# Row-tile sessions: two steps' scores joined round pieces of a plain down projection and round the first two up products of a row block

## The chip, the core and the metric

The kernel runs on one core of a Trainium2 chip. The metric is the device time of one execution in microseconds (us). The kernel before takes 957.05 us, the median of three runs (956.88 to 957.99). All matrices are f32; on the chip an f32 matmul shows as two records.

## The reference, cut to what matters

Routed attention over 4 batches, 8 heads, 768 positions and head size 64, and then a feed-forward block on its output seen as 3072 rows by 512 columns:

```python
q_assign = np.argmax(np.einsum('bhsd,hcd->bhsc', q_n, c_n), axis=-1)   # 16 clusters; q_n, c_n normalised
k_assign = np.argmax(np.einsum('bhsd,hcd->bhsc', k_n, c_n), axis=-1)
mask = q_assign[:, :, :, None] == k_assign[:, :, None, :]
scores = np.where(mask, scale * np.matmul(q, k.transpose(0, 1, 3, 2)), -1000000000.0)
attn = softmax(scores)                     # exp, then division by the sum of the row
x = np.matmul(attn, v)                     # (B,H,S,D), turned into (3072, 512)
h = x @ w_in                               # 512 by 2048
out = (h - np.tanh(h)) @ w_out             # 2048 by 512
```

## The kernel before, in words

**Steps.** The attention is cut into 96 steps, numbered by `at`. A step is a pair of heads `n` (16 pairs, 4 to a batch), a half of the query columns (384) and a third `s` of the key rows (two key tiles of 128). For a step, `begin` (L492) multiplies keys by queries into two `sc` tiles (L499), and ScalarE takes the exponential in place (L521, written back into `sc`). `select` (L524) multiplies each `sc` tile by the cluster mask on VectorE and writes the weights `e` (L531, two instructions to a tile). GpSimd adds the weights up for the softmax's sum (L543, L547). `value` (L549) multiplies values by weights into `av` (L556). After the third step of a half, `take` copies `av` out on ScalarE (L581), and `total` or `total_both` brings the sum onto all partitions with a matmul into `den`. Later `scale` (L692) or `divide` (L707, L710) multiplies the attention's output `xT` by the reciprocal.

**Pieces.** The feed-forward work of an earlier batch is cut into pieces which a planner lays between the steps. Each has a cost, and a step takes pieces off the front of the list `fill` into `now` while the cost spent keeps pace with the steps. Batch 0 is done in two halves by `plain_items`. Its second half (in steps 24 to 47) has up products and then twelve `project` pieces (L746): four quarters `i` of the 2048 rows of `w_out` for each of three row tiles `sub`. Here a piece is written (sub, i). Batches 1 and 2 (steps 48 to 71 and 72 to 95) are done by `strassen_items`: a seven-product scheme with 8 row blocks `i` of 7 up products `k_` (L933, 56 pieces), and then 21 `down_product` pieces (L1038). An up product is written (i, k_). Batch 3 follows behind the last step.

**Shape of the array.** With f32 and two 64-wide halves, most matmuls split the output's 128 columns of the array in two (written 128*64 in the profile: here "column shape"). The scores have only 64 rows to sum over and split the array's rows (64*128: "row shape").

**Sessions.** From step 49 on, at odd steps at which the piece at the head of `now` is a down product, the flag `joint` (L1261) is set. Then `begin` of the next step, `select` of the next step, that down product with its rows split (`rows_=True`: two partial outputs `parts`, one for each 64 rows, added on VectorE at L1044 or L1053) and `begin` of the step after it stand one behind the other. This document calls such a stretch of row-shaped matmuls a session. At all other steps `begin(following)` stands alone, ahead of `value(at)` and the pieces.

**Order.** The kernel writes the order of every engine's work by hand: an instruction's place in its engine's queue is its place in the code. What a step has to do beside its pieces stands in the list `todo`. It holds the `select` of the next step, the transpose `pq` of the cluster codes by TensorE with the copy `qc` (`publish`, L432, L434), the routing of a later pair on VectorE (`similar`, `turn_back`, `route`: L376, L386 to L414), `scale`, and sums of weight quarters (`made`, L831) for the seven-product scheme. The function `between`, called inside each piece, emits a share of it. Where `now` is empty it is emitted at once. `right_factors` (L899) makes the differences `diff` of `xT` at the start of a batch's pieces.

**Buffers.** PSUM has two `sc` tiles of two banks each, one bank for `av` (pool `ps_a`), and three banks in pool `ps_f` for everything else: up products, down products, `den`, `pq`, `sim` and the accumulator of a plain projection, which keeps its bank for four pieces. There are two `e` tiles (`ep`), so that `select` of a step waits for `value` two steps earlier. `row` tiles (the codes spread over the partitions, L454) number three, and weight blocks (`stream`, L853) three. `fetch_factors` asks for a block two blocks ahead, at product (i, 2).

```python
joint = at > 4 * HALF and at % 2 == 1 and at + 2 < len(steps) and now and now[0][1] == 2
...
elif following and at >= NS - 1 and following not in begun:
    begin(following)
```

Of the kernel before, what the change touches and what calls it, by code (L numbers as in the profile page):

```python
# [30 lines left out]
F32 = mybir.dt.float32  # L31
# [4 lines left out]
ALU = mybir.AluOpType  # L36
# [3 lines left out]
P = 128  # L40
# [18 lines left out]
def kernel(  # L59
# [10 lines left out]
    nc = tc.nc  # L70
# [108 lines left out]
    def fast():  # L179
# [539 lines left out]
        def plain_items(half: int):  # L719
            gs, acc = {}, {}  # L720
            sequence = [i * FQ + o for i in ORDER for o in range(FQ)]

            def up(f: int, between):
                i, o = f // FQ, f % FQ
                if f < CF // 2:
                    gs[f] = gp.tile([P, 2, TB], F32, name="g")
                h = ps_f.tile([P, TB], F32, name="h", tag="f")
                for c in range(CD):
                    for r in halves:
                        nc.tensor.matmul(  # L730
                            h[r], lhsT=w_in[i][:, c, o * P : (o + 1) * P][:, r], rhs=xT[c][:, half],
                            start=(c == 0), stop=(c == CD - 1),
                        )
                th = thp.tile([P, TB], F32, name="th")
                nc.scalar.activation(out=th, in_=h, func=ACT.Tanh)
                between()
                nc.vector.tensor_tensor(
                    out=gs[f % HF][:, f // HF], in0=h, in1=th, op=ALU.subtract
                )

            def project(sub: int, i: int, between):
                if i == 0:
                    acc[sub] = ps_f.tile([P, DM], F32, name="o", tag="f")
                for f in sequence[i * FQ : (i + 1) * FQ]:
                    for r in halves:
                        nc.tensor.matmul(  # L746
                            acc[sub][r], lhsT=gs[f % HF][:, f // HF, sub * P : (sub + 1) * P][:, r],
                            rhs=w_out[f // FQ][:, f % FQ],
                            start=(f == sequence[0]), stop=(f == sequence[-1]),
                        )  # L750
                between()
                if i == NQ4 - 1:
                    osb = restp.tile([P, DM], F32, name="osb", tag="rest")
                    nc.scalar.mul(out=osb, in_=acc.pop(sub), mul=float(words))
                    nc.gpsimd.dma_start(out_r[0, half * HCH + sub], osb)

# [9 lines left out]
            return ups + [  # L766
                (3.4 if half == 0 else 3.0, 1, lambda between, s=s, i=i: project(s, i, between)) for s, i in order
            ]


# [130 lines left out]
        def up_items(b: int, base: int, quarter, shrink, done):  # L901
# [2 lines left out]
            held = {}  # L904
            width = TB if b else TB // 2

            def up_product(i: int, k_: int, between):
                which = PRODUCTS[k_]
                x = [columns(b, c) for c in range(CD)]
                d = diffs[b] if which in (4, 5, 6) else None  # L910
# [13 lines left out]
                        held[i] = t[:, 0, 0:width], t[:, 1].rearrange("p (a n) -> p a n", a=2)  # L924
                s, u = held[i]

                def add(out, x, y):
                    nc.vector.tensor_tensor(out=out, in0=x, in1=y, op=ALU.add)  # L928

                ps = ps_f.tile([P, TB], F32, name="pu", tag="f")[:, 0:width]  # L930
                for c in range(CH):
                    for r in halves:
                        nc.tensor.matmul(  # L933
                            ps[r], lhsT=streams[base + i][:, c, k_, r], rhs=right[c],
                            start=(c == 0), stop=(c == CH - 1),
                        )
                if which == 1:
                    nc.scalar.copy(out=s, in_=ps)
                elif which == 2:
                    add(quarter(i, 0, 0), ps, s)  # L940
                    if i == HF - 1:
                        shrink(i, 0, slice(0, 1))
                elif which == 6:
                    fetch_factors(base + i + 2)
                    add(u[:, 0], ps, s)
                elif which == 7:
                    add(u[:, 1], ps, u[:, 0])
                elif which == 4:
                    add(quarter(i, 1, 0), ps, u[:, 1])
                elif which == 5:  # L950
                    add(u[:, 0], ps, u[:, 0])
                    add(quarter(i, 1, 1), ps, u[:, 1])
                    shrink(i, 1, slice(0, 2))
                else:
                    add(quarter(i, 0, 1), ps, u[:, 0])

                    shrink(i, 0, slice(1 if i == HF - 1 else 0, 2))
# [4 lines left out]


            return [
                (1.3 * width / TB, 1, lambda between, i=i, k_=k_: up_product(i, k_, between))
                for i in range(HF) for k_ in range(len(PRODUCTS))
            ]

# [23 lines left out]
        def strassen_items(b: int):  # L992
# [21 lines left out]
            def down_product(k_: int, j: int, between, rows_=False):  # L1014
# [64 lines left out]


            return up_items(b, base, lambda i, f, t: G[:, i, f, t], shrink, done) + [
                (3.4, 2, lambda between, rows_=False, k_=k_, j=j: down_product(k_, j, between, rows_))
                for k_ in range(len(PRODUCTS)) for j in range(HCH)
            ]

# [152 lines left out]
        for at, (n, half, s) in enumerate(steps):  # L1238
# [19 lines left out]

            joint = at > 4 * HALF and at % 2 == 1 and at + 2 < len(steps) and now and now[0][1] == 2  # L1261
            values_first = 1 in stages and not summed(n, half)
            if values_first:
                value(n, half, s)
# [367 lines left out]
```

## Time and profile before

| | |
|---|---|
| median of three runs | 957.05 us |
| the profiled execution's own time | 955.51 us |
| its span (first to last instruction) | 953.65 us, so 1.86 us lie around it |
| granted TensorE clock | 1.00 |
| busy time of PE (TensorE) / DVE (VectorE) | 939.2 / 580.3 us |
| busy time of ACT (ScalarE) / POOL (GpSimd) | 293.5 / 510.5 us |
| score matmuls L499 | 768 records, 149.3 us |
| plain projection L746 | 384 records, 86.1 us |
| up products L933 | 1792 records, 280.1 us |
| down products L1038 | 2016 records, 223.7 us (191.4 and 32.3) |
| PE, longest waits by releaser | 1.6 us on L531, 1.3 on L231, 1.2 on L581 in all |

PE is the matmul part of TensorE, PEld its weight loads. A timeline line has the start and the time taken in us, engine, source line, operation, output and inputs, shapes, the number of instructions merged (x), and in brackets the idle time ahead of it with what ended it.

### The profile page before, as it was taken

How to read it: one execution, taken by the hardware profiler on the slowest of the kernel's cores; microseconds unless marked ns; L12 is line 12 of the kernel's file. 1: busy time of each engine (PE TensorE's matmuls, PEld its weight loads, DVE VectorE, ACT ScalarE, POOL GpSimd, SP SyncE). 2: the span in 40 equal slices, each digit the busy share in tenths (PEclk: the TensorE clock that was granted, in tenths of full speed). 3: DMA queues.
4: the chain of work that ended last, by engine and by line, in shares of the span. 5: the costliest groups of instructions: out<-in, count | busy, mean ns of one | idle time of the engine just before them, and what ended most of it. 6: DMA issues, size and time to landing. Idle time of an engine off the chain costs nothing.

```text
span 953.6 us, 16953 instructions
## 1 busy us (share of the span) xinstructions
PE 939.2 (98%) x6584; PEld 469.0 (49%) x6584; DVE 580.3 (61%) x1111; ACT 293.5 (31%) x453; POOL 510.5 (54%) x364
## 2 busy tenths in 40 slices
PE   8999999999999999999999999999999999999997
PEld 5434443355653334444465665444456665445664
DVE  6647686976776678566845567766656338443011
ACT  5586564223332332323322112333331220222000
POOL 1026353456775465777785453867797343657500
PEclk9999999999999999999999999999999999999999
DMA  7767465892736645474565645557334223323331
GB/s 193 205 182 154 118 172 128 249 278 86 196 116 160 158 136 132 151 180 132 170 170 182 153 152 187 126 184 170 114 128 147 98 84 100 116 78 132 107 106 37
DMA packets 166764, 139.85 MB, mean 147 GB/s; under 512 B 116580, under 2 KB 145044, under 8 KB 163988
## 3 DMA queue, kind: packets, MB, share of 16 engines
q1 hardware_dynamic: 160292, 117.15, 44.7%
q0 software_dynamic: 6240, 21.50, 6.9%
q8 instruction: 54, 0.88, 0.4%
q14 instruction: 34, 0.28, 0.1%
q10 hardware_dynamic: 144, 0.03, 0.0%
HBM read 117.48 MB, written 21.17 MB: 145 GB/s over the span
## 4 chain that ended last, share of the span: by engine, by line
PE 89%; DVE 3%; DMA 2%; ACT 1%; issue 1%; SPq 0%; DVEq 0%; ACTq 0%
PE pu L933 26%; PE pd L1038 22%; PE sc L499 13%; PE av L556 13%; PE o L746 6%; PE h L730 4%; PE sim L376 1%; PE den L617 1%; DVE e L531 1%; DMA stream<-up_factors 1%; PE den L571 1%; DVE diff L899 1%; PE den L590 1%; DVE den L707 1%; DMA row<-q_codes 0%
## 5 line engine op out<-in xcount | busy, mean ns | idle before, releaser
L547 POOL TENSOR_TENSOR sum<-sum,e 128x768 f32<-128x768 f32 x112 | 207.2, 1850 | 99.7 <-DVE e L531 95.4
L531 DVE SCALAR_TENSOR_TENSOR e<-row,code,sc 128x384 f32<-128x384 bf16 x336 | 185.0, 608 | 78.3 <-ACT sc L521 53.2
L1038 PE MATMUL pd<-stream,G 128*64 128x256 f32 (+1 forms) x1728 | 191.4, 378 | 0.0
L521 ACT ACTIVATE sc<-sc 128x768 f32<-128x768 f32 x168 | 126.1, 789 | 191.1 <-PE sc L499 171.9
L1038 PEld LDWEIGHTS pd<-stream,G 128*64 128x64 f32 (+1 forms) x1728 | 131.3, 145 | 60.7 <-issue 5.7
L933 PE MATMUL pu<-xT,stream 128*64 128x384 f32 (+1 forms) x1024 | 159.0, 447 | 0.8 <-PE pu L933 0.4
L499 PE MATMUL sc<-t,t 64*128 64x384 f32 x768 | 149.3, 506 | 0.6 <-ACT e L521 0.3
L556 PE MATMUL av<-e,vals 128*64 128x384 f32 x768 | 145.6, 498 | 2.8 <-DVE e L531 1.6
L1002 POOL TENSOR_TENSOR G<-G,th 128x768 f32<-128x768 f32 (+1 forms) x51 | 87.1, 1723 | 69.4 <-ACT th L1000 69.2
L933 PE MATMUL pu<-diff,stream 128*64 128x384 f32 (+1 forms) x768 | 121.1, 448 | 1.8 <-DVE t L928 1.0
L933 PEld LDWEIGHTS pu<-xT,stream 128*64 128x64 f32 x1024 | 73.2, 137 | 74.7 <-issue 60.4
L499 PEld LDWEIGHTS sc<-t,t 64*128 64x128 f32 x768 | 66.7, 186 | 71.0 <-issue 34.3
L543 POOL TENSOR_TENSOR sum<-e 128x768 f32<-128x768 f32 x28 | 52.6, 1879 | 70.1 <-DVE e L531 57.2
L556 PEld LDWEIGHTS av<-e,vals 128*64 128x64 f32 x768 | 47.2, 136 | 85.0 <-issue 77.3
L1000 ACT ACTIVATE th<-G 128x768 f32<-128x768 f32 (+1 forms) x51 | 40.9, 806 | 148.9 <-DVE G L928 144.2
L746 PE MATMUL o<-w_out,g 128*64 128x512 f32 x384 | 86.1, 593 | 0.0
L933 PEld LDWEIGHTS pu<-diff,stream 128*64 128x64 f32 x768 | 53.8, 137 | 58.3 <-issue 45.4
L928 DVE TENSOR_TENSOR G<-pu,u 128x384 f32<-128x384 f32 x72 | 39.8, 552 | 32.9 <-PE pu L933 32.9
L746 PEld LDWEIGHTS o<-w_out,g 128*64 128x64 f32 x384 | 27.4, 137 | 50.1 <-issue 49.6
L1053 DVE SCALAR_TENSOR_TENSOR c<-pd,du 128x256 f32<-128x256 f32 x36 | 15.1, 419 | 48.8 <-PE pd L1038 48.8
L730 PE MATMUL h<-xT,w_in 128*64 128x384 f32 x256 | 42.8, 486 | 0.0
L1053 DVE SCALAR_TENSOR_TENSOR du<-pd,du 128x256 f32<-128x256 f32 x31 | 13.1, 423 | 48.6 <-PE pd L1038 48.1
(139 smaller groups left out, 835.2 us busy)
## 6 DMA issues: line engine op xcount, KB each, us to landing
stream<-up_factors SPq DMA_DIRECT2D x32, 896.0 KB
stream<-down_factors SPq DMA_DIRECT2D x21, 1024.0 KB
raw<-in_moe_w_in_dram POOLq DMA_DIRECT2D x16, 512.0 KB, 5.2
raw<-in_moe_w_out_dram POOLq DMA_DIRECT2D x16, 512.0 KB, 5.0
again<-in_moe_w_in_dram SPq DMA_DIRECT2D x32, 256.0 KB
again<-in_moe_w_out_dram SPq DMA_DIRECT2D x32, 256.0 KB
vals<-in_v_dram SPq DMA_DIRECT2D x32, 192.0 KB
row<-q_codes SPq DMA_DIRECT2D x29, 192.0 KB
```

The source lines that it names most:

```text
L499: nc.tensor.matmul(sc[i][:, h, 0:TB], lhsT=turned[n, 1][r].rearrange("p a n -> p (a n)")[:, j * P : (j + 1) * P], rhs=turned[n, 0][r, half ...
L521: nc.scalar.activation(out=out, in_=sc[i][:, :, 0:TB], func=ACT.Exp, scale=SCALE)
L531: nc.vector.scalar_tensor_tensor(out=e[:, h].rearrange("p (j n) -> p j n", n=P), in0=rows[n, half][:, h], scalar=(codes[n][:, h, 1, j : j ...
L543: nc.gpsimd.tensor_tensor(out=s, in0=pair[0], in1=pair[1], op=ALU.add)
L547: nc.gpsimd.tensor_tensor(out=s, in0=s, in1=pair[i], op=ALU.add)
L556: nc.tensor.matmul(avs[n, half][h * D : h * D + D], lhsT=vals[n][:, h, j], rhs=e[i][:, h], start=(j == 0), stop=(j == NCH - 1),)
L730: nc.tensor.matmul(h[r], lhsT=w_in[i][:, c, o * P : (o + 1) * P][:, r], rhs=xT[c][:, half], start=(c == 0), stop=(c == CD - 1),)
L746: nc.tensor.matmul(acc[sub][r], lhsT=gs[f % HF][:, f // HF, sub * P : (sub + 1) * P][:, r], rhs=w_out[f // FQ][:, f % FQ], start=(f == seq ...
L933: nc.tensor.matmul(ps[r], lhsT=streams[base + i][:, c, k_, r], rhs=right[c], start=(c == 0), stop=(c == CH - 1),)
L1000: nc.scalar.activation(out=th, in_=t, func=ACT.Tanh)
L1002: nc.gpsimd.tensor_tensor(out=t, in0=t, in1=th, op=ALU.subtract)
L1038: nc.tensor.matmul(out_, lhsT=w, rhs=x, start=(i == 0), stop=(i == HF - 1))
```

## The change

Five things are changed. `project` of the second half of batch 0 can run with its rows split: one partial output stays in the accumulator, the other goes to a bank of its own (`low`) and is added into the SBUF tile `osb` by ScalarE (first time) or VectorE. `up_product` can run with its rows split (`apart`), with two partial outputs that are added one after the other. `joint` is now set by a mark on the piece, which down products and these `project` pieces bear, and no longer from step 49 on alone; a joint step also takes a second piece into `now` where it has only one. New is the list `leads`: at an odd step after 48 whose first piece is an up product, and from which a new row block is near, the first two products of that block are pulled ahead of the others. They run row-shaped, with the two score tiles of the step after next behind the first and the second of them. Last, `spread` of a second half's codes of pairs 4 to 7 is asked for three steps ahead instead of two.

The diff, cut where it only renames:

```diff
-            def project(sub: int, i: int, between):
+            parts_of = {}
+
+            def project(sub: int, i: int, between, rows_=False):
...
+                low = ps_f.tile([P, DM], F32, name="o", tag="f") if rows_ else None
+                fs = sequence[i * FQ : (i + 1) * FQ]
+                for f in fs:
+                    g = gs[f % HF][:, f // HF, sub * P : (sub + 1) * P]
+                    w = w_out[f // FQ][:, f % FQ]
+                    for h, r in enumerate(halves):
+                        alone_ = rows_ and h
                         nc.tensor.matmul(
-                            acc[sub][r], lhsT=gs[f % HF][:, f // HF, sub * P : (sub + 1) * P][:, r],
-                            rhs=w_out[f // FQ][:, f % FQ],
-                            start=(f == sequence[0]), stop=(f == sequence[-1]),
+                            low if alone_ else acc[sub] if rows_ else acc[sub][r],
+                            lhsT=g[r] if rows_ else g[:, r], rhs=w[r] if rows_ else w,
+                            start=(f == (fs if alone_ else sequence)[0]),
+                            stop=(f == (fs if alone_ else sequence)[-1]),
                         )
+
+                def add(ps):
+                    if sub not in parts_of:
+                        parts_of[sub] = restp.tile([P, DM], F32, name="osb", tag="rest")
+                        nc.scalar.mul(out=parts_of[sub], in_=ps, mul=float(words))
+                        return
+                    t = parts_of[sub]
+                    nc.vector.scalar_tensor_tensor(
+                        out=t, in0=ps, scalar=float(words), in1=t, op0=ALU.mult, op1=ALU.add
+                    )
+
+                if rows_:
+                    add(low)
                 between()
                 if i == NQ4 - 1:
-                    osb = restp.tile([P, DM], F32, name="osb", tag="rest")
-                    nc.scalar.mul(out=osb, in_=acc.pop(sub), mul=float(words))
+                    add(acc.pop(sub))
+                    osb = parts_of.pop(sub)
...
-            def up_product(i: int, k_: int, between):
+            def up_product(i: int, k_: int, between, apart=False):
...
+                parts = [
+                    ps_f.tile([P, TB], F32, name="pu", tag="f")[:, 0:width]
+                    for _ in range(2 if apart else 1)
+                ]
+
                 def add(out, x, y):
-                    nc.vector.tensor_tensor(out=out, in0=x, in1=y, op=ALU.add)
-
-                ps = ps_f.tile([P, TB], F32, name="pu", tag="f")[:, 0:width]
+                    for j, part in enumerate(parts):
+                        nc.vector.tensor_tensor(out=out, in0=part, in1=out if j else y, op=ALU.add)
+
+                ps = parts[0]
                 for c in range(CH):
-                    for r in halves:
+                    for h, r in enumerate(halves):
+                        w = streams[base + i][:, c, k_]
                         nc.tensor.matmul(
-                            ps[r], lhsT=streams[base + i][:, c, k_, r], rhs=right[c],
+                            parts[h] if apart else ps[r], lhsT=w[r] if apart else w[:, r],
+                            rhs=right[c][r] if apart else right[c],
                             start=(c == 0), stop=(c == CH - 1),
                         )
                 if which == 1:
                     nc.scalar.copy(out=s, in_=ps)
+                    if apart:
+                        nc.vector.tensor_tensor(out=s, in0=parts[1], in1=s, op=ALU.add)
...
-            joint = at > 4 * HALF and at % 2 == 1 and at + 2 < len(steps) and now and now[0][1] == 2
+            pairable = at != 4 * HALF - 1 and at % 2 == 1 and at + 2 < len(steps) and now
+            joint = pairable and now[0][3:] == (True,)
+            while joint and len(now) < 2 and fill:
+                now.append(fill.pop(0))
+                spent += now[-1][0]
+            leads = []
+            if pairable and at > 4 * HALF and now[0][3:4] == (False,):
+
+
+                blocks = [it[4] for it in now + fill if len(it) > 4]
+                new = [i for i, k_ in blocks if k_ == 0]
+                if new and min(i for i, _ in blocks) >= new[0] - 1:
+                    while (new[0], 1) not in [it[4] for it in now if len(it) > 4]:
+                        now.append(fill.pop(0))
+                        spent += now[-1][0]
+                    leads = [it for it in now if it[4:] in (((new[0], 0),), ((new[0], 1),))]
+                    now = [it for it in now if it not in leads]
+                    while spent > whole * part and len(now) > 1:
+                        fill.insert(0, now.pop())
+                        spent -= fill[0][0]
...
                 if to and to[1] == 1:
-                    kind = 1 if to[0] < HP else 2 if to[0] >= 2 * HP else 0
+                    kind = 1 if to[0] < HP else 2
...
-            if joint:
+            if joint or leads:
...
-                now.pop(0)[2](lambda: None, True)
-                begin(steps[at + 2])
+                if joint:
+                    now.pop(0)[2](lambda: None, True)
+                    begin(steps[at + 2])
+                for i, it in enumerate(leads):
+                    it[2](lambda: None, True)
+                    begin(steps[at + 2], (i,))
+                joint = True
```

More of the change, by code (lines that the diff above doesn't have):

```diff
@@ L739, in up @@
                 )
-            def project(sub: int, i: int, between):
+            parts_of = {}
+            def project(sub: int, i: int, between, rows_=False):
                 if i == 0:
                     acc[sub] = ps_f.tile([P, DM], F32, name="o", tag="f")
-                for f in sequence[i * FQ : (i + 1) * FQ]:
-                    for r in halves:
+                low = ps_f.tile([P, DM], F32, name="o", tag="f") if rows_ else None
[5 more added lines that the diff above has]
+                        alone_ = rows_ and h
                         nc.tensor.matmul(
-                            acc[sub][r], lhsT=gs[f % HF][:, f // HF, sub * P : (sub + 1) * P][:, r],
-                            rhs=w_out[f // FQ][:, f % FQ],
-                            start=(f == sequence[0]), stop=(f == sequence[-1]),
-                        )
+                            low if alone_ else acc[sub] if rows_ else acc[sub][r],
+                            lhsT=g[r] if rows_ else g[:, r], rhs=w[r] if rows_ else w,
+                            start=(f == (fs if alone_ else sequence)[0]),
+                            stop=(f == (fs if alone_ else sequence)[-1]),
+                        )
+                def add(ps):
[9 more added lines that the diff above has]
+                    add(low)
                 between()
                 if i == NQ4 - 1:
-                    osb = restp.tile([P, DM], F32, name="osb", tag="rest")
-                    nc.scalar.mul(out=osb, in_=acc.pop(sub), mul=float(words))
+                    add(acc.pop(sub))
+                    osb = parts_of.pop(sub)
                     nc.gpsimd.dma_start(out_r[0, half * HCH + sub], osb)
@@ L766, in plain_items @@
             return ups + [
-                (3.4 if half == 0 else 3.0, 1, lambda between, s=s, i=i: project(s, i, between)) for s, i in order
+                (
+                    3.4 if half == 0 else 3.0, 1,
+                    lambda between, rows_=False, s=s, i=i: project(s, i, between, rows_), half == 1,
+                )
+                for s, i in order
             ]
@@ L925, in up_product @@
                 s, u = held[i]
+                parts = [
+                    ps_f.tile([P, TB], F32, name="pu", tag="f")[:, 0:width]
+                    for _ in range(2 if apart else 1)
+                ]
                 def add(out, x, y):
-                    nc.vector.tensor_tensor(out=out, in0=x, in1=y, op=ALU.add)
-                ps = ps_f.tile([P, TB], F32, name="pu", tag="f")[:, 0:width]
+                    for j, part in enumerate(parts):
+                        nc.vector.tensor_tensor(out=out, in0=part, in1=out if j else y, op=ALU.add)
+                ps = parts[0]
                 for c in range(CH):
-                    for r in halves:
+                    for h, r in enumerate(halves):
+                        w = streams[base + i][:, c, k_]
                         nc.tensor.matmul(
-                            ps[r], lhsT=streams[base + i][:, c, k_, r], rhs=right[c],
+                            parts[h] if apart else ps[r], lhsT=w[r] if apart else w[:, r],
+                            rhs=right[c][r] if apart else right[c],
                             start=(c == 0), stop=(c == CH - 1),
@@ L964, in up_items @@
             return [
-                (1.3 * width / TB, 1, lambda between, i=i, k_=k_: up_product(i, k_, between))
+                (
+                    1.3 * width / TB, 1,
+                    lambda between, apart=False, i=i, k_=k_: up_product(i, k_, between, apart),
+                    False, (i, k_),
+                )
                 for i in range(HF) for k_ in range(len(PRODUCTS))
@@ L1081, in strassen_items @@
             return up_items(b, base, lambda i, f, t: G[:, i, f, t], shrink, done) + [
-                (3.4, 2, lambda between, rows_=False, k_=k_, j=j: down_product(k_, j, between, rows_))
+                (3.4, 2, lambda between, rows_=False, k_=k_, j=j: down_product(k_, j, between, rows_), True)
                 for k_ in range(len(PRODUCTS)) for j in range(HCH)
```

## The prediction

> **What bounds the kernel now.** I read the page first, busy time and then the chain that ended last:
>
> ```profile
> PE 939.2 (98%) x6584; PEld 469.0 (49%) x6584; DVE 580.3 (61%) x1111; ACT 293.5 (31%) x453; POOL 510.5 (54%) x364
> PE 89%; DVE 3%; DMA 2%; ACT 1%; issue 1%; SPq 0%; DVEq 0%; ACTq 0%
> ```
>
> TensorE is busy for 98% and is 89% of the chain. So a nanosecond between matmuls counts, and so does every wait that TensorE gets. Next comes the timeline of PE round one session of the kernel before, with the ACT and DVE lines that belong to it:
>
> ```profile
> 704.05 1.56 PE L499 MATMUL sc<-t,t 64*128 64x384 f32 x8
> 705.45 3.62 PE L1038 MATMUL pd<-stream,G 64*128 64x256 f32 x32
> 708.90 1.46 PE L499 MATMUL sc<-t,t 64*128 64x384 f32 x8
> 710.29 1.51 PE L556 MATMUL av<-e,vals 128*64 128x384 f32 x8
> ...
> 705.06 1.50 ACT L521 ACTIVATE sc<-sc 128x768 f32<-128x768 f32 x2 [0.51 <-PE sc L499]
> ...
> 705.96 2.19 DVE L531 SCALAR_TENSOR_TENSOR e<-row,code,sc 128x384 f32<-128x384 bf16 x4 [5.12 <-ACT sc L521]
> ```
>
> The eight score records take 1.56 us where the shape has just changed and 1.46 where it has not. Record by record, two concurrent matmuls start every 0.323 us for the scores and the up products, every 0.216 for down products in either shape, and every 0.429 for the plain projection. From column to row shape 0.100 is lost ahead of the first pair and 0.104 behind it; from row to column 0.096 and 0.051. A round trip costs **0.351 us**, and it is not idle time in the page. From the same lines a second clock can be read, which I count from a session's first score matmul: exponential at +1.01, mask at +1.91, first `sc` tile masked (two of four) at +3.05.
>
> **Part 1: fewer changes of shape.** I laid the shapes along TensorE's instruction order of both programs. Column to row falls from 62 to 51, row to column from 81 to 68. There are 13 new sessions: five round `project` (steps 37, 39, 41, 43, 45) and eight round leads (51, 53, 55, 57 and 75, 77, 79, 81). I priced each kind of change by its median in this trace, those from and to the routing's 32-wide shape too (0.10 to 0.31). The sum falls from 37.8 to 33.5 us: **-4.26**. The matmuls keep their number. Row-shaped up products and 512-wide projections are not in the trace. Row and column agree for down products, and the row shape's longer weight load (0.187 against 0.137, L499 and L746) lies under the 0.323 and 0.429 between starts, so I take 0. The other end: 0.05 in each of the 104 new row pairs, +5.2.
>
> **Part 2: a second piece at steps 65 and 89.** There the only piece now goes into the session, and two `value` groups follow each other. The second waits for the single `av` bank to be copied out:
>
> ```profile
> 525.09 1.51 PE L556 MATMUL av<-e,vals 128*64 128x384 f32 x8 [0.58 <-ACT xT L581]
> ```
>
> Record to record this gap is 0.75 over the rhythm, here and at 748.6. With a 3.45 us piece between, the copy (0.48) is hidden: **-1.50**.
>
> **Part 3: the leads, a new wait.** A lead is 4 pairs of 0.323. So TensorE reaches the third `sc` tile at 1.40 + 1.29 = +2.69. That tile is the first one's buffer, free when its mask is done: +3.05, and 0.14 more to the matmul, as this old stall shows (mask halves end at 575.64, matmul at 575.78):
>
> ```profile
> 574.50 2.18 DVE L531 SCALAR_TENSOR_TENSOR e<-row,code,sc 128x384 f32<-128x384 bf16 x4
> 575.78 1.97 PE L499 MATMUL sc<-t,t 64*128 64x384 f32 x8 [0.18 <-DVE e L531]
> ```
>
> So TensorE waits 3.19 - 2.69 = 0.50 where it now waits for nothing. Queued behind it are the second lead, the last `sc` tile and `value`. At steps 51, 57, 75 and 81 the previous step ends with a row block's last product, whose two tanh stand in ScalarE's queue ahead of the exponential:
>
> ```profile
> 384.74 1.67 ACT L1000 ACTIVATE th<-G 128x768 f32<-128x768 f32 x2 [3.72 <-DVE G L928]
> 384.80 1.56 PE L499 MATMUL sc<-t,t 64*128 64x384 f32 x8
> 386.32 1.49 ACT L521 ACTIVATE sc<-sc 128x768 f32<-128x768 f32 x2
> 387.21 1.14 DVE L531 SCALAR_TENSOR_TENSOR e<-row,code,sc 128x384 f32<-128x384 bf16 x2 [1.74 <-ACT sc L521]
> ```
>
> Exponential at +1.52 instead of +1.01, mask done at 387.21 + 1.14 = +3.55, matmul at +3.69: wait 1.00. Sum 4 x 0.50 + 4 x 1.00 = **+6.0**. The fourth tile is no trouble: second mask +4.1 or +4.6, TensorE there at +5.1 or +5.6. Each session saves 0.35, so the leads lose as a whole. The bounds: 0, if the tile is free by +2.69, and +8 at 1.00 each.
>
> The added VectorE work (two instructions of 0.56 to a session) and ScalarE's copy (0.48, over by +3.5; the second lead needs that bank at +4.3) lie beside matmuls; without that cover it would be 16 x 0.56 = 9 us. Weight blocks are asked for at product (i, 2), 12 us ahead of the lead that needs them (25 before); the longest stream load in the chain took 7.2. The earlier `row` request moves one load past `list` and weight-quarter loads on SP's queue, with nothing behind it that is late: 0.
>
> TensorE could only hide this wait by letting the second lead pass. [...]
>
> **Part 4: the project sessions.** A piece is 8 pairs of 0.429, so the third tile is wanted at 1.40 + 3.43 = +4.83 and the fourth at +5.48, against +3.19 and +4.24. A session here waits only if VectorE comes over 1.2 us late to the mask (its normal start is +1.91). The order within two steps is now: session, `value`, a column piece, transposes, `value`; nothing stands beside the second step's `value`. By the lengths in the trace VectorE comes in time at 37, 39, 43, 45. Before 41 it has, from +11.4 after session 39: `qc`, one `made` behind a GpSimd add that ends at 12.7, two L692, two `made`, to 17.2; session 41 starts at +13.6. Mask from +3.6, fourth tile free at +5.95: **+0.5**.
>
> **Part 5: VectorE's run into step 48.** Here VectorE, not TensorE, is late already: it runs unbroken from 342.70 to the first up products, which waited 0.97 us for it at 364.9. Part of this run:
>
> ```profile
> 342.70 0.28 DVE L434 CAST qc<-pq 12x128 bf16<-12x128 f32 x1 [2.58 <-PE pq L432]
> 342.91 2.55 DVE L707 RECIPROCAL den<-den 128x128 f32<-128x128 f32 x3
> ...
> 345.98 2.18 DVE L531 SCALAR_TENSOR_TENSOR e<-row,code,sc 128x384 f32<-128x384 bf16 x4
> 348.07 1.41 DVE L692 TENSOR_TENSOR xT<-xT,den 128x384 f32<-128x384 f32 x1
> 349.41 2.16 DVE L692 TENSOR_TENSOR xT<-xT,t 128x384 f32<-128x384 f32 x1
> 351.50 1.21 DVE L831 TENSOR_TENSOR made<-w_out,made 128x1024 f32<-128x1024 f32 x1
> ...
> 364.33 0.55 DVE L928 TENSOR_TENSOR G<-pu,s 128x384 f32<-128x384 f32 x1
> ```
>
> The run starts when `pq` of step 45 is transposed, 6.67 us after that step's scores (336.03). Now a session's second scores (1.29), then `value`, and piece (2,2) stand ahead of `pq`: 1.40 + 3.43 + 1.29 + 1.44 + 3.43 + 0.1 for the change + 0.3 = 11.4, or +4.75. Against that, the second mask (345.98 to 348.07, 2.1) is done before `qc`. The two L692 (3.43, each beside a GpSimd add; 0.54 where GpSimd was idle, at 568.91) meet only one add, L711: about 1.9, so -1.5. The accumulator's new add is 128x512 on VectorE; from 0.42 at 256 columns and 0.61 at 384 I estimate 0.8. So 4.75 - 2.1 - 1.5 + 0.8 = +1.95, and the 0.2 saved by this stretch's session is swallowed: **+2.1**. Bounds: 0.5 if the run finds slack, 3.6 if GpSimd is met as before.
>
> **Part 6.** In step 69 `pq` also falls behind a piece: `qc` 1.6 us later, 1.2 of it in VectorE's gaps round 570, and the stall at 575.78 grows: **+0.4**.
>
> [...] If each of 13 sessions waited for one copy (0.48, L938), that would be 6.2 us more. I charge nothing: along the bank numbers each bank was left a product or more earlier, and the only late one, the accumulator's before step 48, lies inside part 5.
>
> **Sum.** -4.26 - 1.50 + 6.0 + 0.5 + 2.1 + 0.4 = +3.2 us. The profiled execution (955.51: span 953.65 and 1.86 round it) would be 958.7; the median of 957.05 is 1.54 higher, so I predict **960.3 us**.
>
> **Rivals.** (a) *No wait at the leads* (other side): the first tile is masked by +2.55, so the third is free when wanted. This decides it: below +2.55 the leads gain. For it: only half of the mask has to be done by then; against it: both rows of part 3, +3.05 and +3.55. Price 6.0 off: 954.3. 15%. (b) *Half waits*: 0.5 at all eight leads and VectorE's run finds its slack: -2.0 and -1.9, 956.4, within 0.2%. For it: idle VectorE time near 340; against it: the run's unbroken lines. 25%. (c) *VectorE later*: L692 meets GpSimd as before in parts 4 and 5, 1.4 and 1.5 more, 963.2. 17%. (d) That the change doesn't do what it says: excluded by the order, which has the 13 sessions. My forecast: 43%.
>
> **Numbers.** The measurement can tell 0.2% (1.9 us). Faster by more: (a) and a little of (b), 17%. Within: 26%, (b) and the low edge of the forecast. Slower: 57%. The range of 954.9 to 964.6 leaves out most of (a) and what lies beyond (c), and holds the bounds of parts 3 and 5; the full +5.2 of part 1 lies outside. The forecast's own range is 959 to 962.
>
> **What would show it.** Right: L499 with idle time before it on L531 at eight leads, 0.5 or 1.0 each; no wait on L581 near 525 and 749; the diff products after step 48 waiting longer; 0.1 us less per missing change of shape. Wrong: score matmuls on time in the leads, or row-shaped L746 or L933 pairs further apart than 0.429 and 0.323.

## The result, and the profile after

The changed kernel takes 967.95 us (median of five runs, 966.64 to 972.31) against 957.05 for the kernel before. The ratio is 1.0129, 95% interval 1.0107 to 1.0152: slower by 10 to 15 us, where I had forecast 3 us. The direction was right and the size was not; the range, which ended at 964.6, missed it. The profiled execution is the slowest of the five (972.31, span 970.5), so its sums come out 4.4 above the median.

The page shows TensorE with nearly the same busy time, and its share of the chain of waits down from 89% to 76%. VectorE has risen from 3% to 9%, DMAs from 2% to 6%:

```profile
PE 941.2 (97%) x6584; PEld 478.1 (49%) x6584; DVE 585.4 (60%) x1132; ACT 294.0 (30%) x453; POOL 507.6 (52%) x364
PE 76%; DVE 9%; DMA 6%; ACT 2%; issue 2%; POOL 1%; SPq 1%; DVEq 0%; POOLq 0%; ACTq 0%
```

TensorE's waits by releaser name what stands ahead of it. (Columns: us in total, times, longest; the kernel before first, then the changed kernel.)

```profile
PE sc L499 <- DVE e L531: 0.2, 1, 0.2
...
PE sc L499 <- DVE e L531: 13.7, 12, 3.1
```

Before, score matmuls waited 0.2 us for the mask. Now they wait 13.7 us in twelve places. To see where the time goes I laid the start of the first `av` matmul (L556) of a step in one trace beside that of the same step in the other, at steps where the order of work is the same again:

| step | before | after | later by | since the row above |
|---|---|---|---|---|
| 36 | 277.02 | 279.08 | 2.06 | 2.06, ahead of all sessions |
| 48 | 357.46 | 360.56 | 3.09 | 1.03, five project sessions |
| 50 | 376.91 | 381.30 | 4.39 | 1.30, VectorE's run into step 48 |
| 59 | 460.50 | 469.89 | 9.39 | 5.00, four leads |
| 61 | 485.73 | 494.79 | 9.06 | -0.33 |
| 67 | 539.67 | 548.45 | 8.77 | -0.29, second piece of 61 and 65 |
| 73 | 592.44 | 605.74 | 13.30 | 4.53, second piece of 69 and session 71 |
| 83 | 685.06 | 702.40 | 17.34 | 4.04, four leads |
| 85 | 710.29 | 727.29 | 17.01 | -0.33 |
| 91 | 764.23 | 780.88 | 16.65 | -0.36, second piece of 85 and 89 |

The first 2.06 us are no effect of the change: the twelve variants below have the same code up to step 36, and as profiled they lie there between 1.17 ahead of the kernel before and 1.96 behind it. All of them also ask earlier for `spread`, the fifth part of the change. In e5 steps 36 to 65 take the time of the kernel before to 0.01 us, so it costs nothing there. The -0.33 twice stands at eight sum matmuls (L617), which take 0.85 us at 472.62 and 705.13, and 1.19 and 1.18 in the kernel before (463.23 and 687.79). Its cause is open.

Two leads in TensorE's timeline, steps 51 and 57:

```profile
389.19 1.56 PE L499 MATMUL sc<-t,t 64*128 64x384 f32 x8
390.58 1.46 PE L967 MATMUL pu<-xT,stream 64*128 64x384 f32 x8
392.89 0.92 PE L499 MATMUL sc<-t,t 64*128 64x384 f32 x4 [0.85 <-DVE e L531]
...
448.23 1.50 PE L967 MATMUL pu<-xT,stream 64*128 64x384 f32 x8
451.81 1.15 PE L499 MATMUL sc<-t,t 64*128 64x384 f32 x4 [2.08 <-DVE e L531]
452.69 2.83 PE L967 MATMUL pu<-xT,stream 64*128 64x384 f32 x8
455.25 1.11 PE L499 MATMUL sc<-t,t 64*128 64x384 f32 x4
```

The wait is where the forecast had put it, ahead of the third `sc` tile. In step 51 it is 0.85 us. In step 57 it is 2.08, and behind it the second lead takes 2.83 us instead of 1.49. Its pairs start 0.640 us apart instead of 0.323. The table by windows says why (the third number from the end is the granted clock):

```profile
450.00:452.00 2.00, 0.19 (x2) 0.22 (x4) 1.47 (x3) 1.52 (x3) 2.00 (x2) 1.00 1.08 349
452.00:454.00 2.00, 2.00 (x9) 1.19 (x9) 1.18 (x3) 0.80 (x1) 1.84 (x3) 0.59 0.81 336
454.00:456.00 2.00, 2.00 (x10) 1.17 (x6) 0.51 (x1) 0.00 (x0) 2.00 (x2) 0.56 0.04 16
456.00:458.00 2.00, 2.00 (x15) 0.82 (x14) 0.61 (x2) 0.80 (x1) 1.92 (x2) 1.00 0.03 8
```

After the wait TensorE runs for some 3 us at half its clock (0.50 from 452.37 to 455.78): five pairs start 0.32 further apart each, 1.6 us. It happens again behind the wait of session 71 below (0.72, 0.50 and 0.92 in the two-us windows from 588.00 on).

What made step 57 late stands on VectorE (the first three lines) and ScalarE (the last two):

```profile
445.92 0.42 DVE L1211 TENSOR_REDUCE smallest<-again 128x1 f32<-128x256 f32 x1 [2.12 <-DMA again<-in_moe_w_in_dram]
...
447.51 1.01 DVE L961 TENSOR_TENSOR G<-pu,u 128x384 f32<-128x384 f32 x2
450.53 2.19 DVE L531 SCALAR_TENSOR_TENSOR e<-row,code,sc 128x384 f32<-128x384 bf16 x4 [2.01 <-ACT sc L521]
...
448.15 1.58 ACT L1041 ACTIVATE th<-G 128x768 f32<-128x768 f32 x2 [4.54 <-DVE G L961]
449.63 1.49 ACT L521 ACTIVATE sc<-sc 128x768 f32<-128x768 f32 x2
```

L1211 is a check of weights read a second time (`again`, loaded at L1196); from step 48 on every step has two of them and two loads in its list `todo`, until all 64 are done. VectorE stands 2.12 us at a check whose load has not landed. The last sums `G` of the row block come behind it, and behind those the two tanh, the exponential and the mask. That this check makes the wait is tested in e7.

Session 71 waits 3.07 us. The lines below are, in this order, TensorE's wait, a check and the mask on VectorE, the same check in the kernel before, and what SyncE issues in the changed kernel:

```profile
587.43 2.33 PE L499 MATMUL sc<-t,t 64*128 64x384 f32 x8 [3.07 <-DVE e L531]
...
581.82 0.42 DVE L1211 TENSOR_REDUCE smallest<-again 128x1 f32<-128x256 f32 x1 [1.50 <-DMA again<-in_moe_w_out_dram]
...
586.15 2.19 DVE L531 SCALAR_TENSOR_TENSOR e<-row,code,sc 128x384 f32<-128x384 bf16 x4 [0.90 <-DMA row<-q_codes]
...
571.10 0.42 DVE L1170 TENSOR_REDUCE smallest<-again 128x1 f32<-128x256 f32 x1 [0.98 <-DMA again<-in_moe_w_out_dram]
...
574.87 0.33 SPq L438 DMA_DIRECT2D q_codes<-qc  x1
578.93 0.82 SPq L1196 DMA_DIRECT2D again<-in_moe_w_out_dram  x2
579.84 0.38 SPq L454 DMA_DIRECT2D row<-q_codes  x1
```

Two things make the mask late, and one `again` load is behind both. It waits for a buffer, that is for VectorE's checks at 578.49, which stand behind the reciprocals. VectorE stands 1.50 us at the next check until this load has landed. SyncE issues the `row` load behind it, 4.97 us after the codes (4.31 in the kernel before), and the row lands 6.3 us later; the mask waits 0.90 for it. Counted from step 67 the mask starts 2.9 us later than in the kernel before: 2.0 by VectorE's own queue and 0.9 by the row.

Session 41 is late by the row alone. Its codes were transposed behind a whole piece of step 39 (`pq` at 308.36, in the kernel before at 301.78), and VectorE is idle:

```profile
317.30 1.97 PE L499 MATMUL sc<-t,t 64*128 64x384 f32 x8 [1.33 <-DVE e L531]
...
316.01 2.19 DVE L531 SCALAR_TENSOR_TENSOR e<-row,code,sc 128x384 f32<-128x384 bf16 x4 [1.57 <-DMA row<-q_codes]
```

The scores of step 50 wait for the mask at the end of VectorE's run (reciprocals, `osb`, eight instructions of `right_factors`), which has no check in it:

```profile
370.37 1.97 PE L499 MATMUL sc<-t,t 64*128 64x384 f32 x8 [1.58 <-DVE e L531]
```

### The profile page after: what moved, and what is told of

Read it like the earlier page. It is cut to its first block, busy times and chain, and to the rows that moved or that the text cites. A ratio compares the mean times of both kernels' runs of the same rounds, so it can differ in the third digit from the quotient of the medians.

```text
span 970.5 us, 17000 instructions
## 1 busy us (share of the span) xinstructions
PE 941.2 (97%) x6584; PEld 478.1 (49%) x6584; DVE 585.4 (60%) x1132; ACT 294.0 (30%) x453; POOL 507.6 (52%) x364
## 4 chain that ended last, share of the span: by engine, by line
PE 76%; DVE 9%; DMA 6%; ACT 2%; issue 2%; POOL 1%; SPq 1%; DVEq 0%; POOLq 0%; ACTq 0%
PE pd L1079 22%; PE pu L967 18%; PE sc L499 11%; PE av L556 11%; PE o L755 7%; PE h L730 4%; DVE e L531 3%; DMA den<-back 1%; DMA row<-q_codes 1%; PE sim L376 1%; DMA again<-in_moe_w_out_dram 1%; DMA stream<-up_factors 1%; DVE den L707 1%; DMA again<-in_moe_w_in_dram 1%; POOL G L1043 1%
## 5 line engine op out<-in xcount | busy, mean ns | idle before, releaser
L547 POOL TENSOR_TENSOR sum<-sum,e 128x768 f32<-128x768 f32 x112 | 205.1, 1831 | 111.8 <-DVE e L531 107.5
L499 PE MATMUL sc<-t,t 64*128 64x384 f32 x768 | 152.6, 508 | 14.7 <-DVE e L531 13.7
L967 PE MATMUL pu<-xT,stream 128*64 128x384 f32 (+2 forms) x1024 | 163.0, 450 | 0.6 <-DMA stream<-up_factors 0.4
L556 PE MATMUL av<-e,vals 128*64 128x384 f32 x768 | 146.5, 501 | 1.2 <-DVE e L531 1.2
L967 PE MATMUL pu<-diff,stream 128*64 128x384 f32 (+1 forms) x768 | 121.3, 448 | 1.6 <-DVE t L961 1.0
L967 PEld LDWEIGHTS pu<-xT,stream 128*64 128x64 f32 (+1 forms) x1024 | 78.1, 144 | 70.1 <-issue 48.0
L499 PEld LDWEIGHTS sc<-t,t 64*128 64x128 f32 x768 | 67.8, 187 | 87.1 <-issue 39.1
L556 PEld LDWEIGHTS av<-e,vals 128*64 128x64 f32 x768 | 48.5, 137 | 80.3 <-issue 74.8
L755 PE MATMUL o<-w_out,g 128*64 128x512 f32 (+1 forms) x384 | 86.0, 592 | 0.0
L967 PEld LDWEIGHTS pu<-diff,stream 128*64 128x64 f32 x768 | 54.5, 137 | 58.4 <-issue 41.7
L755 PEld LDWEIGHTS o<-w_out,g 128*64 128x64 f32 (+1 forms) x384 | 29.4, 147 | 48.0 <-issue 46.6
```

Source lines behind the costliest of these rows:

```text
L499: nc.tensor.matmul(sc[i][:, h, 0:TB], lhsT=turned[n, 1][r].rearrange("p a n -> p (a n)")[:, j * P : (j + 1) * P], rhs=turned[n, 0][r, half ...
L547: nc.gpsimd.tensor_tensor(out=s, in0=s, in1=pair[i], op=ALU.add)
L556: nc.tensor.matmul(avs[n, half][h * D : h * D + D], lhsT=vals[n][:, h, j], rhs=e[i][:, h], start=(j == 0), stop=(j == NCH - 1),)
L755: nc.tensor.matmul(low if alone_ else acc[sub] if rows_ else acc[sub][r], lhsT=g[r] if rows_ else g[:, r], rhs=w[r] if rows_ else w, start ...
L967: nc.tensor.matmul(parts[h] if apart else ps[r], lhsT=w[r] if apart else w[:, r], rhs=right[c][r] if apart else right[c], start=(c == 0), ...
```

## The experiments

All were timed beside the kernel before, in three groups; its median in them was 956.45 (e1 to e4), 955.56 (e5 to e8) and 956.46 us (e9 to e12). Theory A was formed from the tables above, theory B is the prediction, theory C puts the loss on the clock alone.

**The parts by themselves**

*e1: without leads.*

```diff
-            if pairable and at > 4 * HALF and now[0][3:4] == (False,):
+            if False:
```

> The changed kernel without the leads; row-split projections and second pieces stay. Theory A (read from the two traces, stage by stage): the leads cost +8.4 us (4.7 in steps 50 to 59, 3.7 in 74 to 83), since the third sc tile came 0.34, 0.34, 0.85 and 2.08 us late in each batch, each with about 0.24 more to start the array again, and only 4 x 0.35 saved. So about 959.6 us, and the 3.2 us wait on L531 in step 71 stays. Theory B (the prediction on record): leads +6.0 - 2.8 = +3.2, so some 965. Theory C: most of the loss is a lowered granted clock that follows any long wait of TensorE; then the clock stays below 1.00 here and the time stays above 963.

Measured: 960.99 us, ratio 1.0055 (1.004 to 1.007). The long wait of step 71 is there (2.6 us). The time is nearest to A, 1.4 above it. C has the clock right (0.995 to 0.998) and the time wrong. In this trace the mask of step 71 does not wait for the row at all. VectorE comes to it late, having stood 1.32 and 0.94 us at two checks:

```profile
575.96 0.42 DVE L1211 TENSOR_REDUCE smallest<-again 128x1 f32<-128x256 f32 x1 [0.94 <-DMA again<-in_moe_w_out_dram]
...
578.62 2.18 DVE L531 SCALAR_TENSOR_TENSOR e<-row,code,sc 128x384 f32<-128x384 bf16 x4
```

*e2: leads alone.*

```diff
-            joint = pairable and now[0][3:] == (True,)
-            while joint and len(now) < 2 and fill:
+            joint = pairable and at > 4 * HALF and now[0][3:] == (True,)
+            while False:
```

> The kernel before with the leads alone (projections and second pieces as before). Theory A: 957.05 + 8.4 = 965.4 us, L499 with idle time on L531 of about 7 us in eight waits, the two longest near 2.1. Theory B: 960.2. Theory C: a clock below 1.00 and above 966.

Measured: 966.02 us, ratio 1.0104 (1.0085 to 1.0124). The eight waits are 0.85, 0.34, 0.35 and 2.04 us, then 0.85, 0.34, 0.35 and 2.08; in step 57 the half clock follows again (0.85 and 0.98 in the ten-us windows from 440 on). Theory A holds, B falls.

*e3: second pieces alone* (e1's edit, and `joint` as in e2).

> The kernel before with the second piece in joint steps alone (no leads, no row-split projections). Theory A: the wait on av goes at steps 65 and 89 (-1.6), but the publishing of the codes falls behind the second piece of step 69, the row of step 72 lands late, and L499 waits 3 us for L531 in step 71: 957.05 - 1.6 + 0.9 + 3.2 to 4.5, 959.5 to 961. Theory B (prediction: -1.5 and +0.4): 956.0. Theory D: the late row in step 71 belongs to that one execution and its DMA, and is not there: 956.4 or less.

Measured: 958.74 us, ratio 1.0021 (1.0003 to 1.0039). L499 waits 2.3 us in step 71, with the clock at 0.93 and 0.90 in the 20 us around it. The mask waits only 0.17 for the row here, so A's reason for the wait is not what this trace shows. D falls: the wait is 3.07, 2.58 and 2.30 us in the three profiles that have the second piece of step 69 as changed, and 0.18 to 0.71 in the kernel before, e2, e4 and e5. It is not the piece alone, though: e7 and e8 lack it and wait 1.36 and 1.83, after VectorE has stood 1.67 and 1.66 us at a check. The median lies 0.8 below A's range.

*e4: project sessions alone* (e1's edit; the `while` of second pieces only for `at < 4 * HALF`).

> The kernel before with row-split projections (and their second pieces) in steps 37 to 45 alone. Theory A: +2.3 us (TensorE waits 1.8 in session 41 and 1.95 before the scores of step 50, against 0.97 before; the round trips save 0.8): 959.4. Theory B (prediction: -1.45 + 0.5 + 2.1): 958.2. In either case no wait on L531 in steps 51 to 95 beyond those of the kernel before.

Measured: 958.52 us, ratio 1.0034 (1.0014 to 1.0053). Steps 36 to 50 lose 2.36 us in the trace, as in the changed kernel (2.33). A and B are too close for the time to part them; the trace has A's waits.

The three parts add up to 9.6 + 2.3 + 2.1 = 14.0 us by medians, inside the 10.2 to 14.5 of the whole.

**Second pieces: what is late in step 71**

*e5: second pieces in two steps* (on top of e3).

```diff
-            while joint and len(now) < 2 and fill:
+            while joint and at in (65, 89) and len(now) < 2 and fill:
```

> The kernel before with a second piece in the joint steps 65 and 89 alone, not in 61, 69, 85 and 93. Theory A (two second pieces gain 0.8 each on the av bank; that of step 61 and of 85 cost 0.5 and 0.4; that of 69 costs the long wait of step 71): 956.45 - 1.6 = 954.9, and step 71 waits 0.65 as in the kernel before. Rival: the long wait of step 71 has another source than step 69's second piece; then it stays at 2 to 3 us and the time is 957 or more.

Measured: 954.41 us, ratio 0.9986 (0.9976 to 0.9996). Step 71 waits 0.41 over the rhythm at its first late tile, before 0.35. In the trace steps 65 to 67 gain 0.81 and steps 89 to 91 gain 0.80.

*e6: the codes published ahead of the second piece* (on top of e3).

```diff
+            if at == 69:
+                stages.pop(3)()
             todo += [stages[i] for i in (5, 3, 4) if i in stages]
```

> As e3 (second pieces in all joint steps), but in step 69 the transpose pq and the copy qc of the codes are emitted ahead of the second piece, where the kernel before has them. Theory A (the wait of step 71 is the row of codes that lands late because pq is late): L531 of step 72 no longer waits for the row, step 71 waits 0.7 or less, 956.45 - 1.6 + 0.9 = 955.8. Rival: the order of the pieces makes VectorE late in step 71, whatever pq does: the wait stays above 2 us and the time near 958.7.

Measured: 956.51 us, ratio 1.0009 (0.9997 to 1.0021): 0.95 above its kernel before, where A has 0.65 below, and in the trace the wait is still 1.6 us. So late `pq` is not the cause by itself, and theory A in this form falls; the rival's 2 us are not reached either. `qc` is now early, but the row is issued 0.74 later than in the kernel before (counted from step 67), behind the `again` loads, and lands 6.2 us after that:

```profile
561.68 0.33 SPq L438 DMA_DIRECT2D q_codes<-qc  x1
567.84 0.81 SPq L1196 DMA_DIRECT2D again<-in_moe_w_out_dram  x2
568.75 0.38 SPq L454 DMA_DIRECT2D row<-q_codes  x1
...
574.96 2.19 DVE L531 SCALAR_TENSOR_TENSOR e<-row,code,sc 128x384 f32<-128x384 bf16 x4 [0.73 <-DMA row<-q_codes]
```

So the next theory was SyncE's queue.

*e10: no checks in step 69; pq stays late* (on top of e3).

```diff
-                todo += [check_done, check_done, check_on, check_on]
+                if at != 69:
+                    todo += [check_done, check_done, check_on, check_on]
```

> As e3 (second pieces in all joint steps), but step 69 issues no checks; pq stays late. Theory A (the row of step 72 is issued late because SyncE stands at a check's load, which waits for VectorE's earlier check behind the reciprocals): the row is issued within 2.5 us of q_codes, L531 does not wait for it, step 71 waits less than 0.7 us, and the time is 1.3 us below the kernel before. Rival: the late pq alone makes the row late: the wait stays above 1.5 us and the time 1 us or more above the kernel before.

Measured: 954.89 us, ratio 0.999 (0.9977 to 1.0002): 1.6 below the kernel before by medians, with an interval that just reaches no change, and clearly below e3. The row is issued 1.28 us after the codes, VectorE does not wait for it, and the late tile of step 71 stands 0.32 over the rhythm:

```profile
566.13 0.33 SPq L438 DMA_DIRECT2D q_codes<-qc  x1
567.41 0.34 SPq L454 DMA_DIRECT2D row<-q_codes  x1
```

The edit also takes checks off VectorE's queue, where e3 stood 1.49 and 0.24 us at two. The run does not part the two effects, but the traces do: the mask waited 0.90 for the row in the changed kernel, 0.17 in e3 and not at all in e1, while TensorE waited 3.07, 2.30 and 2.58. So the larger part was VectorE's checks, and the theory had the right edit for a reason that is the smaller part. In e10 `qc` is still 1.4 us later than in the kernel before (counted from step 67), and yet the mask starts on time.

**Leads: what the wait is made of**

*e7: leads alone, no checks in steps 56 and 80* (the edit of e10 with these two steps).

> As e2 (leads alone), but steps 56 and 80 issue none of the checks (L1196, L1211); the same checks are made in later steps. Theory A (in steps 57 and 81 VectorE stands at a check whose load is late, ahead of the last diff products of a row block, so that the tanh, the exponential and the mask come 1.2 late): the wait in these two falls from 2.08 to 0.85, the time from 966.0 to 963.5. Rival: the two tanh in ScalarE's queue make the wait by themselves, and it stays at 2.08 and 966.

Measured: 960.47 us, ratio 1.0053 (1.004 to 1.0066), against 966.02 for e2. The waits in 57 and 81 are both 0.84:

```profile
446.57 0.92 PE L499 MATMUL sc<-t,t 64*128 64x384 f32 x4 [0.84 <-DVE e L531]
```

So the checks of steps 56 and 80 make the excess of these two waits; what is left is the wait of steps 51 and 75. That is 2.4 us less waiting, but the medians differ by 4.7 (each against its own kernel before). The profile of e7 has no window of half clock, and the mean granted clock of its runs is 0.997 to 1.000 (median 0.9985) against 0.996 to 0.999 (0.997) in e2, worth 1.4 us more. The traces agree: steps 50 to 59 and 73 to 83 lose 8.4 us in e2 and 4.1 in e7, which is 2.4 of waiting, 1.7 of half clock and little else. The leads of four steps now cost 2.03 us in the trace (steps 50 to 59), and that can be summed. There are 2.38 us of idle time. Each of the four waits costs 0.24 more to start again: 0.08 in the first pair, and 0.16 since idle time counts from a matmul's end at 0.483 and the next could have started at 0.323. An up product in step 56 that waits for VectorE's routing adds 0.50. Taken off are 0.39 for an old stall that is gone and 4 x 0.351 for the round trips. The sum is 2.05.

*e8: the exponential writes e directly.* In a lead's step the following step's exponential goes into `e`, and the mask is applied there, so that `sc` is free sooner.

```diff
-                if summed(n, half):
+                if summed(n, half) or step in direct:
                     if i == 0:
                         weights[n, half, s] = weight_tiles(n, half, s)
...
-                sc = e if summed(n, half) else scores.pop((n, half, j))
+                sc = e if summed(n, half) or direct_ else scores.pop((n, half, j))
...
+                if leads:
+                    direct.add(following)
                 begin(following)
```

> As e2 (leads alone), but the exponential of the step after a lead's step is written straight into e and masked there, so that an sc tile is free when its exponential is done and not when its mask is. Theory A (the wait for the third tile is the cost of a lead): no wait in six leads, 0.85 in steps 57 and 81 at most; 966.0 - 7.1 = 958.9. Rival 1: the mask now reads two operands from SBUF beside GpSimd's adds and becomes 1.4 us instead of 0.6, av waits for it, 963 or more. Rival 2: the row-split products themselves or the lowered clock cost the time, and it stays near 966.

Measured: 966.35 us, ratio 1.0103 (1.009 to 1.0117): no gain at all. The wait left the third tile and came back one product later. (PE's timeline, DVE's, and POOL's; lines are shifted by up to 3: L978 is L975, L970 is L967.)

```profile
392.32 1.51 PE L559 MATMUL av<-e,vals 128*64 128x384 f32 x8
395.01 1.51 PE L970 MATMUL pu<-diff,stream 128*64 128x384 f32 x8 [1.18 <-DVE s L978]
...
389.17 5.31 DVE L534 SCALAR_TENSOR_TENSOR e<-row,code,e 128x384 f32<-128x384 bf16 x4 [1.74 <-ACT e L523]
394.40 0.55 DVE L978 TENSOR_TENSOR s<-pu,s 128x384 f32<-128x384 f32 x1
...
387.62 3.90 POOL L1046 TENSOR_TENSOR G<-G,th 128x768 f32<-128x768 f32 x2
391.61 1.19 POOL L1051 TENSOR_TENSOR S<-G 128x384 f32<-128x384 f32 x1
```

Four masks take 5.31 us instead of 2.19 while GpSimd works, 1.33 each. In the kernel before, twelve instructions of the same form (`e<-row,code,e`) take 6.46 us at 22.04, 0.54 each, and GpSimd has no addition beside them, only a cast of 0.18 us and two DMA requests. The lead's own addition (394.40) stands behind the four masks, and until it is done the bank of its second partial output is not free. So rival 1 is right, in its mask though not in the place of the wait. Row-split products thus had a second price here, the bank of the second partial output: six waits of 1.18 to 1.41 us.

**Putting it together**

*e9: the whole change, no checks in steps 56, 69 and 80* (the edit of e10 with these).

> The changed kernel whole, but steps 56, 69 and 80 issue none of the checks (L1196, L1211); the same checks are made in later steps. Theory A (the part of the loss that was not forecast comes from checks in VectorE's and SyncE's queues ahead of the masks of steps 57, 71 and 81, and from the lowered clock that such long waits bring): leads cost +4.9 as in e7 instead of +9.6, and step 71 waits less than 1 us: 967.95 - 4.7 - 2.5 = 960.8, clock 0.998 or more. Rival: the lowered clock comes with row-split products or with second pieces as such: clock 0.997 and 965 or more.

Measured: 960.73 us, ratio 1.0051 (1.0038 to 1.0064). That is theory A's time. The 10.9 us above the kernel before have become 4.3 by moving the checks of three steps to later ones. The clock is 0.997 to 0.999, in part below what A had. One half-clock stretch is left in its profile (0.97 and 0.86 in the ten-us windows from 360 on), behind the wait ahead of step 50 (1.59 us), which has nothing to do with checks.

*e11: project sessions in 37, 39 and 43 only* (e1's edit; second pieces in these three steps alone).

```diff
-            joint = pairable and now[0][3:] == (True,)
+            joint = pairable and (at > 4 * HALF or at in (37, 39, 43)) and now[0][3:] == (True,)
```

> As e4 (row-split projections alone), but only in steps 37, 39 and 43; 41 and 45 stay as in the kernel before. Theory A (the loss of e4 is VectorE late in sessions 41 and in step 49): neither wait is there, three sessions save 0.16 each, and the time is 0.5 us below the kernel before. Rival: the row-split projections cost by themselves (the added copy and additions): 1 us above the kernel before or more.

Measured: 955.87 us, ratio 1.0002 (0.9991 to 1.0014). The time can't tell 0.5 us from nothing. In the trace steps 36 to 50 gain 0.29, step 41 has 0.2 left and the scores of step 50 do not wait, so the loss of e4 is gone.

*e12: what gained, together* (e1's edit, e11's, second pieces in 65 and 89, no checks in step 69).

> The parts that gained, together: second pieces in 65 and 89, row-split projections in 37, 39 and 43, no checks in step 69, no leads. Theory A: -1.6 - 0.5 - 0.6 = 2.7 us below the kernel before. Rival: the gains do not add, since the wait moves to the next late row or check: 1 us below at most.

Measured: 952.79 us, ratio 0.9965 (0.995 to 0.998), 3.7 below its kernel before and faster than both kernels. The trace gains 2.9 between steps 36 and 91, near theory A's 2.7. PE's share of the chain is 89% again.

## Why the prediction was wrong

**What failed is the size of two terms, parts 3 and 6**, and behind both stand the checks in VectorE's queue, with SyncE's loads for them, which I had not followed.

- **Part 3** ("Sum 4 x 0.50 + 4 x 1.00 = +6.0", with bounds "+8 at 1.00 each"). The mechanism, the place and six of the eight waits are right: 0.34 and 0.85 us of idle time, 0.58 and 1.09 with the restart, against 0.50 and 1.00. In steps 57 and 81 it was 2.08, 2.32 with the restart, since the row block's last sums came late behind a check (e7). I had taken step 51's order of tanh and exponential for all four steps and not looked at what stands ahead of the sums. All eight make 9.1. At none of the eight did the second lead pass the wait: in step 57 it starts at 452.69, behind the third `sc` tile's matmuls at 451.81. The upper bound was no bound, as it held the longest wait that I had seen. By medians the leads cost 9.6 us (e2), where I had +6.0 less 2.8 for the shapes.
- **Part 6** ("1.2 of it in VectorE's gaps round 570, and the stall at 575.78 grows: +0.4"). The delay of `qc` was nearly right (1.4 us against 1.6). The step that failed is that the gaps would swallow it. They are waits for the checks' loads (0.98 us at 571.10), and such a load is asked for only when VectorE has done the checks before it (SyncE's L1196 waited for L1211 in 41 places of the changed kernel). So the gap came later together with VectorE, and grew (1.50). The row, behind the same load, came later too. The stall grew by 2.9 us in the changed kernel (2.4 in e1, 2.1 in e3), and steps 67 to 73 lost 4.5 there, 2.4 in e1 and 3.5 in e3, where a half clock is in the first and the last. e10 shows that the checks of step 69 decide it, e6 that the place of `pq` alone does not.
- **No term** stood for the clock. The trace of before shows it at 1.00 everywhere, so it could not be priced from there. In the changed kernel's profile two half-clock stretches cost 1.7 us each.
- **Part 4** (+0.5 at session 41, VectorE late by L692): it was 1.8, and for another reason. The two L692 took 0.55 each and VectorE was idle; what was late was the row, whose `pq` fell behind a piece of step 39.
- **Part 5** (+2.1): it was 1.30, and at another place, the scores of step 50 instead of the diff products.
- **Part 1** (-4.26): the leads saved 0.35 each as priced (e7's sum). The five project sessions saved 0.79 (1.03 less 1.82 for session 41's wait) and not 1.45. Row-shaped pairs are no slower: 0.429 for `project`, 0.323 for up products.
- **Part 2** (-1.50): it was -1.61 (e5). The second of its two waits stands at 749.65 in the trace, not at 748.6. The second pieces of steps 61 and 85, which I had not priced, take back 0.54 and 0.40 (e3).

Rival (c) put the loss on VectorE being late, but through GpSimd at L692; its price did not reach either. That e9 comes out at 960.73, near the forecast, is partly chance, since parts 1, 4 and 5 are off in both directions and the kernel before ran 0.6 us faster beside it.

What stays open is how much of the loss in the executions without a profile was half clock, and how far the two tanh and the checks' loads vary from one execution to the next.

## What to carry to other kernels

When a change makes TensorE wait for a buffer, follow every queue that stands ahead of its release, back to the loads: here checks for which TensorE had not waited became the bound (2.12 us ahead of step 57, 1.50 ahead of session 71), since they stood ahead of results that were now wanted a few us earlier or produced later. A session is worth 0.35 us at most here, so it pays only where the piece between is longer than the mask behind the scores: a down product or a projection of 3.4 us, and not an up product of 1.3. Test the parts alone before giving up a change: second pieces gained in two of their six places (65, 89), lost in three (61, 69, 85) and changed nothing at 93.

## What the runs showed of the hardware

Some waits of TensorE cost more than their length here. In five places the granted clock fell behind one: after waits of 2.08 and 3.07 us (the changed kernel), 2.04 (e2), 2.3 (e3) and 1.59 (e9). In the changed kernel it was 0.50 from 452.37 to 455.78 and from 588.90 to 592.31. By the windows of ten us each took some 1.7 us of clock, and behind other waits of about the same length the clock stayed at 1.00:

| wait | its length in us | granted clock in the ten-us windows round it |
|---|---|---|
| changed kernel, step 57 | 2.08 | 0.83 (450 to 460) |
| changed kernel, step 71 | 3.07 | 0.94 and 0.88 (580 to 600) |
| e2, step 57 | 2.04 | 0.85 and 0.98 (440 to 460) |
| e3, step 71 | 2.3 | 0.93 and 0.90 (570 to 590) |
| e9, step 50 | 1.59 | 0.97 and 0.86 (360 to 380) |
| changed kernel, step 81 | 2.08 | 1.00 |
| e2, step 81 | 2.08 | 1.00 |
| e1, step 71 | 2.6 | 1.00 |
| e4, step 50 | 1.6 | 1.00 |

So the length of a wait alone does not tell the two kinds apart. What does is not shown by these runs.
